# A fused attention and feed-forward kernel: the first two units' scores by head, on 64 rows each, into two PSUM banks, from one smaller load each

## The chip, the core and the metric

The kernel runs on one core of a Trainium2 chip. The core has five engines that run side by side: TensorE for matrix products (PE in the profile, PEld for its loading of the stationary operand), VectorE (DVE), ScalarE (ACT), GpSimd (POOL), and SyncE (SP), whose queue issues nearly all transfers here. Sixteen DMA engines move data between the device memory and SBUF, the on-chip memory. TensorE writes its results into PSUM, eight banks of 512 fp32 numbers on each of 128 partitions; VectorE and ScalarE read them from there.

The metric is the device time of one execution in microseconds (us).

## The reference

Two parts, one after the other. Local attention with memory keys: 4 x 8 heads of 768 tokens and 64 features; each chunk of 32 queries sees 16 tokens to the left of the chunk, the chunk, 8 to the right, and 8 memory keys, so 64 keys.

```python
for c in range(nc):
    ...
    k_full = np.concatenate([mem_k, k_ctx], axis=2)
    v_full = np.concatenate([mem_v, v_ctx], axis=2)
    scores = scale * np.matmul(q_c, k_full.transpose(0, 1, 3, 2))
    scores = scores - np.max(scores, axis=-1, keepdims=True)
    a = np.exp(scores)
    a = a / (np.sum(a, axis=-1, keepdims=True) + 1e-09)
    out[:, :, c_start:c_end] = np.matmul(a, v_full)
```

Then a feed-forward layer over the 3072 tokens of 512 features, with a hidden width of 2048:

```python
h = x @ w_in
g = np.maximum(h, 0.0) + alpha * np.minimum(h, 0.0)
return (g @ w_out).astype(np.float32)
```

All in fp32. At the two ends of a sequence the missing neighbours are left out of the context.

## The kernel before

**Units.** The attention is cut into 32 units: a unit is 384 tokens (half of a sequence, twelve chunks of 32 queries) of one pair of heads. Units 0 to 3 are the four pairs of the first 384 tokens, units 4 to 7 those of the next 384; a unit of the first kind has 16 keys to the left of its first chunk that do not exist, one of the second kind 8 to the right of its last.

**The feed-forward part** works on seven blocks of 384 or 512 tokens. For each block and each of 16 slices of the hidden width (`f`) it multiplies up into `h_ps` (`up`, L741), bends (`below`, `bend`, `high`, `low`) and multiplies down into `o_ps` (`down`, L771). Weights come as 512 KB loads per slice and side and are decoded on ACT, DVE and POOL into a high and a low part (`decode_part`, L638 to L667), since every product is made of three fp32r products. Blocks 0 and 1 are taken in turns while the weights arrive.

**The front.** The first eight units have a path of their own, `windows(u)`: products of queries and keys into PSUM (`score_products`, L317), then on DVE the mask of the missing keys (a memset to -3e38, L520 or L522), the maximum (L524), the subtraction into `e` (L528); the exponential on ACT (L532); the sum and its inverse on DVE (L536, L539); the weights on POOL into `ew` (L549, L553); the turn by TensorE transposes (L561), two copies on ACT (L566), the products with the values (`values`, L574), and the split into a high and a low part (L479 on ACT, L482 on DVE), which are the `up` products' operands. Later units go through `head_products` (L342), which takes the two heads apart: 48 matmuls of 64 rows, two heads in two banks.

In `score_products` one matmul serves both heads: 32 query columns on 128 rows against 2 x 64 keys, where each head's keys are zero on the other head's rows. So a unit's tile `early` is laid out with the keys of one head, the queries, the keys of the other, and it must hold zeros beside the keys. For unit 0 the zeros come with the load, `whole`, 736 KB. For units 1 to 7 they are written by memsets at the start (L211 on POOL, L212 on DVE), and each head comes as a load of 232 KB, `heads`. The values follow as a load of 256 KB each.

**Fillers.** `stir` (L304) issues bf16 products on a constant tile into the unit's score bank ahead of the scores: 8 for unit 0, 2 each for units 1 and 2.

**PSUM.** The eight banks are tiles of pools, allocated anew for each use under a tag: `h0`, `h1`, `o0`, `o1`, `o2`, `s0`, `s1`, `a`. Unit u of the front has its scores in bank `s0` or `s1`, its values' products in `a` or `o2`.

**The order** on each engine is worked out when the program is built, by a list scheduler (`Plan`). Each step has an engine, an estimated cost, what it reads and writes, and a latest-start measure (`rest`); among the steps that could start next on an engine, the one with the longest work behind it goes first. `SHIFT` adds a number of microseconds to that measure for single steps, by their number: a positive one makes the step more urgent. The numbers count the steps in the order in which they are added: the loads of the eight units first (with `al` and `rise`, the slopes' small load and the tile 1 - alpha), then the weights of slices 0 to 7, then the windows of the eight units with 14 steps each, then the rest. On SP a step is a load, so the order among loads comes from there as well.

Of the kernel before, what the change touches and what calls it, by code (L numbers as in the profile page):

```python
# [18 lines left out]
P = 128  # L19
# [82 lines left out]
FIRST_FRONT = 12  # L102


STIR = (8, 2, 0, 0)

DUE_WEIGHTS, LAST_OUT = 4, 8

# [7 lines left out]

NAPART = 2


GATHER_ACT, HIGH_ACT = range(2, 14), 24  # L120


SHIFT = {9: -2.0, 11: 0.6, 18: -3.9, 21: -5.1, 24: 1.4, 25: 3.7, 54: -1.6, 82: 5.1, 87: 1.5, 94: -7.3, 108: 9.2, 136: -11.9, 183: -7.7, 189: -8.2, 192: -9.9, 210: 5.4, 227: 0.7, 228: 3.4}


class Plan:
# [55 lines left out]


@with_exitstack
def body(ctx: ExitStack, tc: tile.TileContext, qvw, kw, whole, heads, w_in, w_out, alpha, out):
    nc = tc.nc
    ctx.enter_context(tc.manual_schedule())
    NKB, NPT, NA = 2, 2, 2
# [11 lines left out]
    ps_h = ctx.enter_context(tc.tile_pool(name="ps_h", bufs=1, space=bass.MemoryType.PSUM))  # L200
    ps_o = ctx.enter_context(tc.tile_pool(name="ps_o", bufs=1, space=bass.MemoryType.PSUM))
    ps_s = ctx.enter_context(tc.tile_pool(name="ps_s", bufs=1, space=bass.MemoryType.PSUM))
    ps_a = ctx.enter_context(tc.tile_pool(name="ps_a", bufs=1, space=bass.MemoryType.PSUM))

    al = const.tile([P, NF], F32, name="al")
    rise = const.tile([P, NF], F32, name="rise")
    busy = const.tile([P, DM], BF16, name="busy")
    nc.vector.memset(busy, 1.0)
    early = [wps[NF - NSET + i, 0].tile([P, NHEAD + NKEYS + NV], F32, name="early", tag="w") for i in range(NSET)]
    for t in early[1:]:  # L210
        nc.gpsimd.memset(t[:, :NKEYS], 0.0)  # L211
        nc.vector.memset(t[:, NHEAD:NHEAD + NKEYS], 0.0)  # L212
    qk = [const.tile([P, BT + NT * NKT], F32, name=f"qk{i}") for i in range(NKB)]
# [92 lines left out]
    def score_products(u):  # L306
        blk, pr = divmod(u, NPAIR)
        st = state[u]
        s_ps = ps_s.tile([P, 512], F32, name="s_ps", tag=f"s{u % 2}")
        stir(s_ps, STIR[0] if u == 0 else STIR[1] if u < 3 else STIR[2])  # L310
        st["s"] = s_ps[:, :2 * NJ * KW].rearrange("p (n k) -> p n k", k=KW)
        t = early[u % NSET]
        q = t[:, NKEYS:NHEAD].rearrange("p (c q) -> p c q", q=CH)
        for j in range(NJ):
            for t4 in range(NT):
                keys = t[:, t4 * NKT + STARTS_WIN[j]:]
                nc.tensor.matmul(  # L317
                    out=st["s"][t4 * CH:(t4 + 1) * CH, 2 * j:2 * j + 2],
                    lhsT=q[:, t4 * NJ + j],
                    rhs=bass.AP(keys.tensor, keys.offset, [keys.ap[0], (NHEAD, 2), (1, KW)]),  # L320
                    start=True, stop=True,
                )

    def banks(us):

        n = len(us)
        ss = [ps_s.tile([P, 512], F32, name="s_ps", tag=f"s{h2}")[:, :n * NJ * KW].rearrange("p (u n k) -> p u n k", u=n, n=NJ)
              for h2 in range(2)]
# [98 lines left out]
    def bank(u):  # L427


        h2 = u % 2  # L430
        if u >= NU - 2:
            return ps_s, f"s{h2}", ("s", h2)
        if h2 or u >= 6 * NPAIR:
            return ps_h, f"h{h2}", f"h{h2}"
        return ps_a, "a", "a"

    def value_products(u):
        st = state[u]
        pool, tag, _ = bank(u)
        st["a"] = pool.tile([P, 512], F32, name="a_ps", tag=tag)  # L440
        for t in range(NT):
            for h2 in range(2):
                nc.tensor.matmul(  # L443
                    out=st["a"][h2 * D:(h2 + 1) * D, t * TQ:(t + 1) * TQ],
                    lhsT=st["v"][:, t, h2, :],
                    rhs=pts[u % NPT][:, :, t, h2, :],
                    start=True, stop=True,
                )
# [41 lines left out]
    def load_first(u):  # L490
        blk, pr = divmod(u, NPAIR)
        t = early[u % NSET]

        def load_whole():
            nc.sync.dma_start(out=t[:, :NHEAD + NKEYS], in_=whole)

        def load_head(h2):
            nc.sync.dma_start(out=t[h2:P:2, h2 * NKEYS:h2 * NKEYS + NHEAD], in_=heads[u, h2])

        def load_values():  # L500
            nc.sync.dma_start(out=t[:, NHEAD + NKEYS:], in_=qvw[blk, pr, :, BT:])

        state[u] = {}
        if u == 0:
            step(SP, 1.88, load_whole, writes=[("fk", u % NSET, 0), ("fk", u % NSET, 1)], rest=due(u))
        else:
            for h2 in range(2):
                step(SP, 0.62, partial(load_head, h2), writes=[("fk", u % NSET, h2)], rest=due(u))
        step(SP, 0.78, load_values, writes=[("fv", u % NSET)], rest=due(u))

    def windows(u):
# [4 lines left out]

        def top():
            s = st["s"]
            if u // NPAIR % 2 == 0:
                nc.vector.memset(s[0:CH, 0:2, 0:LEFT], NEG)  # L520
            else:
                nc.vector.memset(s[3 * CH:4 * CH, 2 * NJ - 2:2 * NJ, KW - NM - RIGHT:KW - NM], NEG)  # L522
            st["mx"] = sm.tile([P, NJ * 2, 1], F32, name="mx", tag=f"mx{u % 3}")
            nc.vector.tensor_reduce(out=st["mx"], in_=s, axis=AX.X, op=ALU.max)  # L524

        def less():
            st["e"] = es[u % 2][:, :, :KW]
            nc.vector.tensor_tensor(out=st["e"], in0=st["s"], in1=st["mx"].broadcast_to([P, NJ * 2, KW]),  # L528
                                    op=ALU.subtract)

        def exps():
            nc.scalar.activation(out=st["e"], in_=st["e"], func=AF.Exp, scale=SCALE)  # L532
# [7 lines left out]

        def scale(part):

            e = st["e"].rearrange("p (j h) k -> p h j k", h=2)
            den = st["den"].rearrange("p (j h) x -> p h j x", h=2)
            ew = ews[u % NPT]
            if part == 0:
                out = ew.rearrange("p h j k -> p h (j k)")[:, :, :2 * (P + CH)]
                out = out.rearrange("p h (j k) -> p h j k", j=2)[:, :, :, :KW]
                nc.gpsimd.tensor_tensor(out=out, in0=e[:, :, :2], in1=den[:, :, :2].broadcast_to([P, 2, 2, KW]),  # L549
                                        op=ALU.mult)  # L550
                return
            for lo, hi, at_ in ((0, KW - NM, P - KW + NM), (KW - NM, KW, CH)):
                nc.gpsimd.tensor_tensor(out=ew[:, :, 2, at_:at_ + hi - lo], in0=e[:, :, 2, lo:hi],  # L553
                                        in1=den[:, :, 2].broadcast_to([P, 2, hi - lo]), op=ALU.mult)
# [11 lines left out]
            nc.scalar.copy(out=et[:, h2], in_=st["t"][h2][:, :NJ * P])  # L566

        def values():
            pool, tag = (ps_o, "o2") if u % 2 else (ps_a, "a")
            st["a"] = pool.tile([P, 512], F32, name="a_ps", tag=tag)  # L570
            v = early[u % NSET][:, NHEAD + NKEYS:].rearrange("p (t h d) -> p t h d", t=NT, h=2)
            for t in range(NT):
                for h2 in range(2):
                    nc.tensor.matmul(  # L574
                        out=st["a"][h2 * D:(h2 + 1) * D, t * TQ:(t + 1) * TQ],
                        lhsT=v[:, t, h2, :],
                        rhs=st["et"][:, h2, :, t, :],
                        start=True, stop=True,
                    )
# [3 lines left out]
        step(DVE, 0.66, top, writes=[sk, ("mx", u % 3)])  # L583
        step(DVE, 0.55, less, reads=[sk, ("mx", u % 3)], writes=e_keys(u))
# [119 lines left out]
    def hidden(blk, f, first_f, last_f):  # L704
# [219 lines left out]
    plan.send()  # L924


_ORDER = ["qvw", "kw", "whole", "heads", "w_in", "w_out", "alpha"]


def _layout(q, k, v, mem_k, mem_v, moe_w_in, moe_w_out, moe_alpha):  # L930
# [7 lines left out]
    def keys(x, mem, s, *spans):  # L938
# [42 lines left out]
```

## Time and profile before

| | |
|---|---|
| device time, median of 3 runs | 597.28 us (596.87 to 597.48) |
| the profiled execution's own time | 596.39 us |
| its span, first to last instruction | 594.5 us |
| granted TensorE clock, mean | 0.999 |
| busy, share of the span | PE 99%, PEld 85%, DVE 66%, ACT 35%, POOL 8% |
| chain that ended last, by engine | PE 96%, DVE 2%, issue 1%, POOL 1% |
| moved by DMA | 47.65 MB, mean 80 GB/s |
| DMA's share by fortieths of the span, the first five | 0.8, 0.9 or more, 0.9 or more, 0.9 or more, 0.3 |

How to read it. A row of a group or of the timeline names a line of the kernel, an engine, an operation, and output and input by the program's names; a row of the chain of work gives start, length, and what ran. Busy time is engine time; what stands in brackets behind a timeline row is how long the engine was idle before it and what ended that. Waits are inferred from semaphores, POOL's spans are rough, and a few records of matmuls can be missing.

### The profile page before, as it was taken

The numbers are of one execution on the slowest core, as the hardware profiler recorded it, in microseconds if no ns is written. First come the engines' busy times: TensorE is split into PE (matmuls) and PEld (weight loads), VectorE is DVE, ScalarE is ACT, GpSimd is POOL, SyncE is SP. The second block draws the span as 40 slices with busy tenths as digits, with TensorE's granted clock in tenths as the row PEclk, the third lists the DMA queues.
The fourth block names the chain that finished last, engine by engine and source line by source line (L and its number), as shares of the span: only waits on it lengthen the run. The fifth ranks groups of instructions, "written<-read, shape, count | busy, mean of one in ns | idle before, by whom it ended". The sixth has DMA issues, their size and how long they took to land.

```text
span 594.5 us, 10993 instructions
## 1 busy us (share of the span) xinstructions
PE 587.2 (99%) x4411; PEld 503.1 (85%) x4412; DVE 391.3 (66%) x907; ACT 208.1 (35%) x578; POOL 48.4 (8%) x74
## 2 busy tenths in 40 slices
PE   7999999999999999999999999999999999999997
PEld 4789998888998989989898888888888888888886
DVE  7989899787869768686895842851961771530530
ACT  3778788625131504424224202302400401210201
POOL 5740000011000101010010100100100100000000
PEclk9999999999999999999999999999999999999999
DMA  8999300222040211403304003003101000000001
GB/s 319 388 408 407 130 0 2 66 65 89 2 153 18 85 59 43 153 1 101 101 0 154 1 1 100 2 0 120 53 1 36 0 1 36 36 1 0 2 0 71
DMA packets 21187, 47.65 MB, mean 80 GB/s; under 512 B 2576, under 2 KB 5904, under 8 KB 21136
## 3 DMA queue, kind: packets, MB, share of 16 engines
q1 hardware_dynamic: 20992, 46.83, 22.1%
q8 instruction: 34, 0.56, 0.4%
q14 instruction: 17, 0.14, 0.1%
q10 hardware_dynamic: 144, 0.13, 0.1%
HBM read 40.66 MB, written 6.29 MB: 79 GB/s over the span
## 4 chain that ended last, share of the span: by engine, by line
PE 96%; DVE 2%; issue 1%; POOL 1%; ACT 0%; POOLq 0%; ACTq 0%
PE h_ps L741 45%; PE o_ps L771 44%; PE a_ps L443 3%; PE s_ps L342 2%; PE s_ps L304 1%; PE a_ps L574 1%; DVE den L536 0%; DVE mx L524 0%; POOL ew L553 0%; PE s_ps L317 0%; DVE e L528 0%; PE o_ps L561 0%; POOL ew L549 0%; DVE w_t L646 0%; DVE a L654 0%
## 5 line engine op out<-in xcount | busy, mean ns | idle before, releaser
L741 PE MATMUL h_ps<-xh,w 128*128 128x384 f32 (+1 forms) x896 | 248.9, 359 | 0.0
L741 PEld LDWEIGHTS h_ps<-xh,w 128*128 128x128 f32 x896 | 164.9, 188 | 16.0
L771 PE MATMUL o_ps<-w,gh 128*128 128x512 f32 x528 | 162.8, 390 | 0.0
L741 PE MATMUL h_ps<-xl,w 128*128 128x384 f32 (+1 forms) x448 | 162.6, 363 | 0.0
L750 ACT ACTIVATE g<-h_ps 128x384 f32<-128x384 f32 (+1 forms) x112 | 60.5, 540 | 195.1 <-PE h_ps L741 128.3
L753 DVE SCALAR_TENSOR_TENSOR g<-g,rise,h_ps 128x384 f32<-128x384 f32 (+1 forms) x112 | 74.7, 668 | 73.1 <-ACT g L750 72.2
L771 PEld LDWEIGHTS o_ps<-w,gh 128*128 128x128 f32 x528 | 99.1, 188 | 20.4
L418 DVE STREAM_TRANSPOSE pt<-e 32x192 f32<-32x192 f32 (+1 forms) x336 | 99.4, 301 | 7.5 <-POOL e L397 2.0
L771 PE MATMUL o_ps<-w,gl 128*128 128x512 f32 x264 | 102.9, 390 | 0.0
L741 PEld LDWEIGHTS h_ps<-xl,w 128*128 128x128 f32 x448 | 84.1, 188 | 10.0 <-DVE xl L482 0.2
L771 PE MATMUL o_ps<-w,xh 128*128 128x512 f32 x240 | 74.9, 393 | 0.0
L771 PEld LDWEIGHTS o_ps<-w,gl 128*128 128x128 f32 x264 | 49.6, 188 | 10.2
L482 DVE TENSOR_TENSOR xl<-a_ps,xh 128x384 fp32r<-128x384 f32 x32 | 17.6, 555 | 59.9 <-ACT xh L479 59.2
L397 POOL TENSOR_TENSOR e<-e,den 128x384 f32<-128x384 f32 x24 | 22.3, 930 | 406.8 <-DVE den L394 267.9
L771 PEld LDWEIGHTS o_ps<-w,xh 128*128 128x128 f32 x240 | 45.0, 188 | 8.9
L759 DVE CAST gh<-g 128x512 fp32r<-128x512 f32 (+1 forms) x72 | 29.0, 403 | 30.7 <-PE o_ps L771 28.1
L479 ACT CAST xh<-a_ps 128x384 fp32r<-128x384 f32 x32 | 14.9, 481 | 95.9 <-PE a_ps L443 93.5
L763 DVE TENSOR_TENSOR gl<-g,gh 128x512 fp32r<-128x512 f32 (+1 forms) x72 | 46.9, 653 | 1.7
L771 PE MATMUL o_ps<-w,xl 128*128 128x512 f32 x120 | 46.8, 390 | 0.0
L376 ACT ACTIVATE e<-s_ps,mx 128x64 f32<-128x64 f32 x144 | 43.2, 317 | 9.6 <-DVE mx L368 9.6
L376 ACT ACTIVATION_READ_ACCUMULATOR e<-s_ps,mx 128x1 f32 x144 | 30.4, 211 | 0.0
L828 ACT COPY o_t<-o_ps 128x512 f32<-128x512 f32 x21 | 12.2, 588 | 44.6 <-PE o_ps L771 44.2
(61 smaller groups left out, 384.4 us busy)
## 6 DMA issues: line engine op xcount, KB each, us to landing
w_t<-w_in SPq DMA_DIRECT2D x16, 512.0 KB, 10.1
w_t<-w_out SPq DMA_DIRECT2D x16, 512.0 KB, 10.2
qk<-kw SPq DMA_DIRECT2D x24, 272.0 KB, 4.3
v_t<-qvw SPq DMA_DIRECT2D x24, 256.0 KB, 2.8
out<-o_t SPq DMA_DIRECT2D x23, 256.0 KB, 2.0
qk<-qvw SPq DMA_DIRECT2D x24, 192.0 KB, 4.6
early<-heads SPq DMA_DIRECT2D x14, 232.0 KB, 4.8
early<-qvw SPq DMA_DIRECT2D x8, 256.0 KB, 5.7
```

Source lines behind the costliest of these rows:

```text
L376: nc.scalar.activation(out=st["e"][:, i], in_=st["s"][h2][:, n], func=AF.Exp, scale=SCALE, bias=d["mx"][:, u - us[0], n, h2:h2 + 1], accum ...
L397: nc.gpsimd.tensor_tensor(out=st["e"], in0=st["e"], in1=st["den"].broadcast_to([P, NJ * 2, KW]), op=ALU.mult)
L418: nc.vector.transpose(out=pts[u % NPT][quad * CH:(quad + 1) * CH, j, t0:t0 + n1 - n0].rearrange("p t h q -> p (t h) q"), in_=(st["e"], zer ...
L443: nc.tensor.matmul(out=st["a"][h2 * D:(h2 + 1) * D, t * TQ:(t + 1) * TQ], lhsT=st["v"][:, t, h2, :], rhs=pts[u % NPT][:, :, t, h2, :], sta ...
L479: nc.scalar.copy(out=ring[k][0][:, cols], in_=st["a"][:, :BT])
L482: nc.vector.tensor_tensor(out=ring[k][1][:, cols], in0=st["a"][:, :BT], in1=ring[k][0][:, cols].bitcast(F32), op=ALU.subtract)
L741: nc.tensor.matmul(out=h["ps"][:, :n_cols], lhsT=ws[f, 0][:, wk, k * P:(k + 1) * P], rhs=parts(blk, k)[1](xk), start=(k == 0 and n == 0), ...
L750: nc.scalar.activation(out=h["g"], in_=h["ps"][:, :n_cols], func=AF.Relu, scale=-1.0)
L753: nc.vector.scalar_tensor_tensor(out=h["g"], in0=h["g"], scalar=rise[:, f:f + 1], in1=h["ps"][:, :n_cols], op0=ALU.mult, op1=ALU.add)
L759: copy(out=h["gh"], in_=h["g"])
L763: nc.vector.tensor_tensor(out=h["gl"], in0=h["g"], in1=h["gh"].bitcast(F32), op=ALU.subtract)
L771: nc.tensor.matmul(out=o_ps[tt], lhsT=h[gk][:, tt * P:(tt + 1) * P], rhs=ws[f, 1][:, wk], start=(f == first_f and i == 0), stop=(f == last ...
```

## The change

Units 0 and 1 get scores by head. Their tile holds queries (384 columns) and keys (544 columns) of head 0 on rows 0 to 63 and of head 1 on rows 64 to 127, in one load of 464 KB each (`firsts`); no zeros are needed, so the two memsets for unit 1's tile go. `pair_products` runs 48 matmuls on 64 rows, head h of unit u into bank u + 2h of one tile.

That tile, `sums`, keeps four banks for the whole program in place of the tags `s0`, `s1`, `a` and `o2`; the pool `ps_a` is gone. So the scores of unit 0 lie in the banks 0 and 2 (formerly `s0` and `a`), those of unit 1 in 1 and 3 (`s1` and `o2`). The mask of the missing left keys is written into all four banks once, before anything else, and the matmuls of a unit's first chunk leave these 16 columns alone; so units 0 and 1 have no memset ahead of their maximum. In `e`, heads now come outermost, for all eight units of the front.

The fillers go to bank `h0`, and unit 0 has five in place of eight. `rise` is computed on POOL in place of DVE. The list of shifts is a new one; as steps are counted, unit 1 has one step fewer, so the same step's number is lower by one. Counted in the new numbers: the weights of slice 0 (24, 25) and the first of slice 1 (26) get +4.3, +3.2, +2.1, where before only the first had one, of +3.7; the values of units 3, 4 and 5 (11, 14, 17) get -4.2, -3.1, -2.5, where before those of units 2, 5 and 6 had -2.0, -3.9, -5.1. The others are for single steps of the windows, of the decode and of the first slices.

```diff
-STIR = (8, 2, 0, 0)
+STIR = (5, 2, 0, 0)
...
+NAPAIR = 2
...
-SHIFT = {9: -2.0, 11: 0.6, 18: -3.9, 21: -5.1, 24: 1.4, 25: 3.7, 54: -1.6, 82: 5.1, 87: 1.5, 94: -7.3, 108: 9.2, 136: -11.9, 183: -7.7, 189: -8.2, 192: -9.9, 210: 5.4, 227: 0.7, 228: 3.4}
+SHIFT = {11: -4.2, 14: -3.1, 17: -2.5, 24: 4.3, 25: 3.2, 26: 2.1, 86: -13.2, 112: 3.2, 187: 3.3, 191: -8.6, 205: 8.0, 218: 1.7, 219: -1.3, 235: -2.0, 241: 8.2}
...
-    ps_a = ctx.enter_context(tc.tile_pool(name="ps_a", bufs=1, space=bass.MemoryType.PSUM))
...
-    for t in early[1:]:
+    sums = ps_s.tile([P, 4, DM], F32, name="sums")
+    S0, S1, A, O2 = range(4)
+    nc.vector.memset(sums[0:CH, :, :LEFT], NEG)
+    for t in early[NAPAIR:]:
         nc.gpsimd.memset(t[:, :NKEYS], 0.0)
         nc.vector.memset(t[:, NHEAD:NHEAD + NKEYS], 0.0)
...
     def score_products(u):
         blk, pr = divmod(u, NPAIR)
         st = state[u]
-        s_ps = ps_s.tile([P, 512], F32, name="s_ps", tag=f"s{u % 2}")
-        stir(s_ps, STIR[0] if u == 0 else STIR[1] if u < 3 else STIR[2])
-        st["s"] = s_ps[:, :2 * NJ * KW].rearrange("p (n k) -> p n k", k=KW)
+        num = STIR[0] if u == 0 else STIR[1] if u < 3 else STIR[2]
+        if num:
+            stir(ps_h.tile([P, 512], F32, name="h_ps", tag="h0"), num)
+        if u < NAPAIR:
+            return pair_products(u)
+        s = sums[:, u % 2, :2 * NJ * KW].rearrange("p (n k) -> p n k", k=KW)
+        st["s"] = s.rearrange("p (j h) k -> p h j k", h=2)
...
+    def pair_products(u):
+
+        st = state[u]
+        t = early[u]
+        st["s"] = sums[:, u % 2::2, :NJ * KW].rearrange("p h (j k) -> p h j k", k=KW)
+        for j in range(NJ):
+            for t4 in range(NT):
+                c, k = t4 * NJ + j, BT + t4 * NKT + STARTS_WIN[j]
+                lo = LEFT if c == 0 else 0
+                for h2 in range(2):
+                    rows = slice(h2 * D, (h2 + 1) * D)
+                    nc.tensor.matmul(
+                        out=st["s"][t4 * CH:(t4 + 1) * CH, h2, j, lo:],
+                        lhsT=t[rows, c * CH:(c + 1) * CH],
+                        rhs=t[rows, k + lo:k + KW],
+                        start=True, stop=True,
+                    )
...
-        def load_whole():
-            nc.sync.dma_start(out=t[:, :NHEAD + NKEYS], in_=whole)
+        def load_both():
+            nc.sync.dma_start(out=t[:, :NHEAD], in_=firsts[u])
...
-        if u == 0:
-            step(SP, 1.88, load_whole, writes=[("fk", u % NSET, 0), ("fk", u % NSET, 1)], rest=due(u))
+        if u < NAPAIR:
+            step(SP, 1.2, load_both, writes=[("fk", u % NSET, 0), ("fk", u % NSET, 1)], rest=due(u))
...
-            if u // NPAIR % 2 == 0:
-                nc.vector.memset(s[0:CH, 0:2, 0:LEFT], NEG)
-            else:
-                nc.vector.memset(s[3 * CH:4 * CH, 2 * NJ - 2:2 * NJ, KW - NM - RIGHT:KW - NM], NEG)
+            if u // NPAIR % 2:
+                nc.vector.memset(s[3 * CH:4 * CH, :, NJ - 1, KW - NM - RIGHT:KW - NM], NEG)
+            elif u >= NAPAIR:
+                nc.vector.memset(s[0:CH, :, 0, 0:LEFT], NEG)
...
-            nc.vector.tensor_tensor(out=st["e"], in0=st["s"], in1=st["mx"].broadcast_to([P, NJ * 2, KW]),
-                                    op=ALU.subtract)
+            nc.vector.tensor_tensor(out=st["e"].rearrange("p (h j) k -> p h j k", h=2), in0=st["s"],
+                                    in1=st["mx"].broadcast_to([P, 2, NJ, KW]), op=ALU.subtract)
...
-            pool, tag = (ps_o, "o2") if u % 2 else (ps_a, "a")
-            st["a"] = pool.tile([P, 512], F32, name="a_ps", tag=tag)
+            st["a"] = sums[:, O2 if u % 2 else A]
...
-        step(PE, 1.33 if u < 3 else 0.8, partial(score_products, u), reads=[("fk", u % NSET, h2) for h2 in range(2)], writes=[sk],
+        step(PE, 1.33 if u < 3 else 0.8, partial(score_products, u), reads=[("fk", u % NSET, h2) for h2 in range(2)],
+             writes=[sk] + ([("a", ("o", 2))[u % 2]] if u < NAPAIR else []),
              rest=due(u))
...
-            step(DVE, 0.1, partial(nc.vector.tensor_scalar, out=rise, in0=al, scalar1=-1.0, scalar2=1.0, op0=ALU.mult,
+            step(POOL, 0.2, partial(nc.gpsimd.tensor_scalar, out=rise, in0=al, scalar1=-1.0, scalar2=1.0, op0=ALU.mult,
```

More of the change, by code (lines that the diff above doesn't have):

```diff
@@ L184, in body @@
 @with_exitstack
-def body(ctx: ExitStack, tc: tile.TileContext, qvw, kw, whole, heads, w_in, w_out, alpha, out):
+def body(ctx: ExitStack, tc: tile.TileContext, qvw, kw, firsts, heads, w_in, w_out, alpha, out):
     nc = tc.nc
@@ L317, in score_products @@
                 nc.tensor.matmul(
-                    out=st["s"][t4 * CH:(t4 + 1) * CH, 2 * j:2 * j + 2],
+                    out=s[t4 * CH:(t4 + 1) * CH, 2 * j:2 * j + 2],
                     lhsT=q[:, t4 * NJ + j],
@@ L322, in score_products @@
                 )
+    def pair_products(u):
[14 more added lines that the diff above has]
+                    )
     def banks(us):
         n = len(us)
-        ss = [ps_s.tile([P, 512], F32, name="s_ps", tag=f"s{h2}")[:, :n * NJ * KW].rearrange("p (u n k) -> p u n k", u=n, n=NJ)
+        ss = [sums[:, h2, :n * NJ * KW].rearrange("p (u n k) -> p u n k", u=n, n=NJ)
               for h2 in range(2)]
@@ L431, in bank @@
         if u >= NU - 2:
-            return ps_s, f"s{h2}", ("s", h2)
+            return None, h2, ("s", h2)
         if h2 or u >= 6 * NPAIR:
             return ps_h, f"h{h2}", f"h{h2}"
-        return ps_a, "a", "a"
+        return None, A, "a"
     def value_products(u):
@@ L439, in value_products @@
         pool, tag, _ = bank(u)
-        st["a"] = pool.tile([P, 512], F32, name="a_ps", tag=tag)
+        st["a"] = pool.tile([P, 512], F32, name="a_ps", tag=tag) if pool else sums[:, tag]
         for t in range(NT):
@@ L518, in top @@
             s = st["s"]
-            if u // NPAIR % 2 == 0:
-                nc.vector.memset(s[0:CH, 0:2, 0:LEFT], NEG)
-            else:
-                nc.vector.memset(s[3 * CH:4 * CH, 2 * NJ - 2:2 * NJ, KW - NM - RIGHT:KW - NM], NEG)
-            st["mx"] = sm.tile([P, NJ * 2, 1], F32, name="mx", tag=f"mx{u % 3}")
+            if u // NPAIR % 2:
+                nc.vector.memset(s[3 * CH:4 * CH, :, NJ - 1, KW - NM - RIGHT:KW - NM], NEG)
+            elif u >= NAPAIR:
+                nc.vector.memset(s[0:CH, :, 0, 0:LEFT], NEG)
+            st["mx"] = sm.tile([P, 2, NJ, 1], F32, name="mx", tag=f"mx{u % 3}")
             nc.vector.tensor_reduce(out=st["mx"], in_=s, axis=AX.X, op=ALU.max)
@@ L541, in scale @@
         def scale(part):
-            e = st["e"].rearrange("p (j h) k -> p h j k", h=2)
-            den = st["den"].rearrange("p (j h) x -> p h j x", h=2)
+            e = st["e"].rearrange("p (h j) k -> p h j k", h=2)
+            den = st["den"].rearrange("p (h j) x -> p h j x", h=2)
             ew = ews[u % NPT]
@@ L568, in values @@
         def values():
-            pool, tag = (ps_o, "o2") if u % 2 else (ps_a, "a")
-            st["a"] = pool.tile([P, 512], F32, name="a_ps", tag=tag)
+            st["a"] = sums[:, O2 if u % 2 else A]
             v = early[u % NSET][:, NHEAD + NKEYS:].rearrange("p (t h d) -> p t h d", t=NT, h=2)
@@ L579, in values @@
                     )
-        step(PE, 1.33 if u < 3 else 0.8, partial(score_products, u), reads=[("fk", u % NSET, h2) for h2 in range(2)], writes=[sk],
+        step(PE, 1.33 if u < 3 else 0.8, partial(score_products, u), reads=[("fk", u % NSET, h2) for h2 in range(2)],
+             writes=[sk] + ([("a", ("o", 2))[u % 2]] if u < NAPAIR else []),
              rest=due(u))
-        step(DVE, 0.66, top, writes=[sk, ("mx", u % 3)])
-        step(DVE, 0.55, less, reads=[sk, ("mx", u % 3)], writes=e_keys(u))
+        also = [("a", ("o", 2))[u % 2]] if u < NAPAIR else []
+        step(DVE, 0.56 if u < NAPAIR else 0.66, top, writes=[sk, ("mx", u % 3)] + also)
+        step(DVE, 0.55, less, reads=[sk, ("mx", u % 3)] + also, writes=e_keys(u))
         step(ACT, 0.52, exps, writes=e_keys(u))
@@ L766, in down @@
             if f == first_f:
-                banks = ([(ps_o, f"o{i}") for i in range(NTT)] + [(ps_a, "a")])[:n_tiles] if not joint else [(ps_s, "s0"), (ps_s, "s1"), (ps_a, "a")]
-                o_ps.extend(pool.tile([P, DM], F32, name="o_ps", tag=tag) for pool, tag in banks)
+                banks = [(ps_o, "o0"), (ps_o, "o1"), (None, O2), (None, A)][:n_tiles] if not joint else [(None, S0), (None, S1), (None, A)]
+                o_ps.extend(pool.tile([P, DM], F32, name="o_ps", tag=tag) if pool else sums[:, tag] for pool, tag in banks)
             for tt in tts:
@@ L924, in body @@
     plan.send()
-_ORDER = ["qvw", "kw", "whole", "heads", "w_in", "w_out", "alpha"]
+_ORDER = ["qvw", "kw", "firsts", "heads", "w_in", "w_out", "alpha"]
 def _layout(q, k, v, mem_k, mem_v, moe_w_in, moe_w_out, moe_alpha):
@@ L951, in _layout @@
                       np.concatenate([qfirst[:, 1], kfirst[:, 1]], axis=2)], axis=1)
-    whole = np.zeros((D, 2, NHEAD + NKEYS), q.dtype)
-    for h in range(2):
-        whole[:, h, h * NKEYS:h * NKEYS + NHEAD] = heads[0, h]
+    firsts = np.concatenate([qfirst.reshape(NWIN, P, BT), kfirst.reshape(NWIN, P, NKEYS)], axis=2)[:NAPAIR]
     vparts = vwin.reshape(NHALF, NPAIR, P, NV)
@@ L958, in _layout @@
         kw=np.ascontiguousarray(kwin).reshape(NHALF, NPAIR, P, NT, NKT),
-        whole=whole.reshape(P, NHEAD + NKEYS),
+        firsts=firsts,
         heads=heads,
```

## The prediction, as it was made before the change had run

> **What bounds the kernel now.** I read the page first, then busy times by stage, then the chain of work that ended last over its first 30 us, then the order of time there, and last the loads.
>
> ```profile
> span 594.5 us, 10993 instructions
> ...
> PE 587.2 (99%) x4411; PEld 503.1 (85%) x4412; DVE 391.3 (66%) x907; ACT 208.1 (35%) x578; POOL 48.4 (8%) x74
> ```
>
> ```profile
> 0.00:5.05 5.05, 3.60 (x8) 1.04 (x8) 3.71 (x8) 1.28 (x1) 4.45 (x16) 1.00 0.61 207
> 5.05:10.00 4.95, 4.22 (x91) 2.74 (x96) 3.72 (x12) 1.25 (x3) 1.42 (x3) 1.00 0.98 345
> 10.00:15.00 5.00, 4.03 (x75) 2.91 (x68) 4.46 (x12) 3.10 (x8) 2.32 (x6) 1.00 1.04 408
> 15.00:20.00 5.00, 4.79 (x100) 3.60 (x96) 4.57 (x14) 3.40 (x8) 3.51 (x7) 1.00 1.00 361
> 20.00:25.00 5.00, 4.78 (x74) 4.07 (x65) 4.52 (x12) 3.70 (x9) 4.18 (x9) 1.00 1.02 391
> 25.00:30.00 5.00, 4.86 (x45) 4.17 (x42) 4.90 (x12) 4.72 (x13) 3.74 (x8) 1.00 1.02 412
> 30.00:35.00 5.00, 5.00 (x51) 4.26 (x50) 3.65 (x6) 3.97 (x8) 2.61 (x3) 1.00 1.03 406
> ```
>
> A stage row gives, after the stage and its length, busy time of PE, PEld, DVE, ACT and POOL, then granted clock, DMA share and GB/s. PE idles 594.5 - 587.2 = 7.3 us in all. Of these 1.45 lie in the first stage and 0.73 + 0.97 + 0.21 + 0.22 + 0.14 = 2.27 in the next five; from 30 us on it has no gap, and the other 3.6 us are the last store. What follows the front is a fixed stream of products, so a change to the first units is worth what it lets that stream start sooner, and no more. In the front three things run close together: DMA is full from 5 us on, DVE nine tenths busy from 10 us on, and PE. The chain there:
>
> ```profile
> 1.45 3.60 PE s_ps L304 x8
> 5.06 1.18 PE s_ps L317 x24
> ...
> 7.91 0.34 DVE mx L524
> ...
> 10.74 0.47 DVE mx L524
> ```
>
> PE carries it through the scores of units 0 and 1, then DVE from maximum to maximum.
>
> **The change, part by part.** In order of time, in brackets what the engine waited for; the last row is the load's size and its time from issue to landing.
>
> ```profile
> 0.73 0.38 SPq L495 DMA_DIRECT2D early<-whole  x1
> ...
> 5.06 0.92 PEld L317 LDWEIGHTS s_ps<-early 128*32 128x32 f32 x24 [0.92 <-DMA early<-whole]
> ...
> 6.18 0.61 PE L304 MATMUL s_ps<-busy 128*128 128x512 bf16 x2
> 6.36 0.09 DVE L520 MEMSET s_ps<- 32x32 f32 x1 [0.94 <-PE s_ps L317]
> 6.48 0.56 DVE L524 TENSOR_REDUCE mx<-s_ps 128x6 f32<-128x384 f32 x1
> ...
> 9.61 0.86 PE L317 MATMUL s_ps<-early 128*32 128x128 f32 x24 [0.52 <-DMA early<-heads]
> ...
> 12.46 0.86 PE L317 MATMUL s_ps<-early 128*32 128x128 f32 x24 [0.96 <-DMA early<-heads]
> early<-whole SPq DMA_DIRECT2D x1, 736.0 KB, 4.3
> ```
>
> *The first load* shrinks from 736 to 464 KB, 278.5 thousand bytes less. At the 345 to 412 GB/s of the stages above that is 0.81 to 0.68 us; I take 0.73. It landed at 0.73 + 4.3 = 5.03, and PE's first scores started on it at 5.06; after, they start at 4.33. Bounds: nothing, if start-up and not bytes sets the landing, and 4.3 x 272/736 = 1.59 us, if all of it scales; I keep near the rate, as DMA runs full soon after. The Trainium skill's page "DMA: Bandwidth & Descriptors", section "Anatomy of one DMA — SWDGE (gpsimd) path", has a fit of 2.0 us plus bytes over 436 GB/s. The 4.3 us here is above its 3.7 for 736 KB; by its slope the gain would be an estimated 0.64 in place of 0.73.
>
> *Unit 1's load* has the bytes of its two old ones and goes right behind the first. So all loads behind them, in a full queue, land about 0.73 sooner too, among them those of units 3 and 4, for which PE waited at 9.61 and 12.46.
>
> *The products.* For units 0 and 1, 24 matmuls on 128 rows become 48 on 64 rows. The later units run that form already:
>
> ```profile
> 108.35 1.24 PE L342 MATMUL s_ps<-qk 64*32 64x64 f32 x96
> 109.52 0.45 PE L741 MATMUL h_ps<-xl,w 128*128 128x384 f32 x1
> ...
> L317 PE MATMUL s_ps<-early x192: 271/273/421, 5.1 to 20.0; 128*32 128x128 f32 x192
> L304 PE MATMUL s_ps<-busy x11: 380/634/635, 1.5 to 7.7; 128*128 128x512 bf16 x11
> ```
>
> Two units take 109.52 - 108.35 = 1.17 us, 0.585 each. Unit 0 of the old form took 1.18 where unit 3's took 0.86: its matmuls reach 421 ns against a median of 273, and the fillers 634 against 380, while the granted clock reads 1.00 in these stages. So PE runs slow for its first four us, whatever that column says, and unit 0's 48 matmuls, all of them now in that time, take twice 0.585 = 1.17. Unit 1 takes 0.585 where the old form took about 0.86.
>
> *The mask.* One memset of four banks at the start, ahead of everything and under the wait for the load, replaces the one ahead of unit 0's and of unit 1's maximum (6.36 to 6.48, so 0.12 each). Unit 0's products end at 4.33 + 1.17 = 5.50; with the 0.18 that stands between 6.18 and 6.36 its maximum starts at 5.68 against 6.48: **0.80 us**. For unit 1, DVE does unit 0's maximum and subtraction first (some 0.59 each) until 6.86, while PE does two fillers (0.61) and the products (0.585) by 6.7; so 6.87 against 7.91: **1.04 us**.
>
> *Fillers.* Eight become five, at 0.45 each (3.60 for eight): they end at 3.7, and PE idles 0.6 until the load, which comes last anyway: nothing. Were the load to land before 3.7, they would be what is late next. In bank h0 they wait for no subtraction any more; that gain lies beside DVE's work.
>
> *From unit 2 on* DVE goes on by its own work, 1.04 sooner. Unit 3's scores waited for their load until 9.61 and ended at 10.47, 0.27 ahead of the maximum at 10.74; a load 0.73 sooner so allows 1.0 at most. Unit 4's load allows PE 0.73 at 12.46, and what PE lacks there it makes up from its waits behind, 0.21 us in the next stage. I take **0.95** carried to 20 us; bounds 0.73 and 1.04 by the same rows.
>
> ```profile
> 25.03 0.45 DVE L173 TENSOR_SCALAR rise<-al 128x16 f32<-128x16 f32 x1
> L553 POOL TENSOR_TENSOR ew<-e,den 128x16 f32<-128x16 f32 x8 | 1.9, 232 | 0.0
> ```
>
> *`rise`* leaves DVE (0.45) for POOL, where the row of that size says 0.23. DVE is 98% busy in that stage, but PE lacks only 0.14 us: I take **0.1**, bounds 0.45 and -0.23 (POOL late with the weights for a turn, on which PE waits).
>
> *Memsets of `early`:* one on DVE and one on POOL go, in the time in which DVE came to wait 0.94 for the scores: nothing on the path; they clear the way for unit 2's loads.
>
> *The kept tile, heads outermost in `e`, new operand patterns:* as many elements and instructions as before; zero. A view over banks 0 and 2 could tie unit 0 to bank 1: a rival.
>
> *The shifts* move weights 0 and 1 ahead on SP's queue and the values of units 3, 4 and 5 back; later ones reorder steps of the decode. No row prices an order. I take zero, with up to 1.1 us either way, half of the 2.27 that PE idles.
>
> Sum: 0.95 + 0.1 = 1.05 us. The profiled execution took 596.39 (its span of 594.5 and 1.9 around it), 0.9 under the median of 597.28; I carry the difference over: 597.28 - 1.05 = **596.2**.
>
> **The rivals.**
>
> *More than that (17%).* With loads and DVE ahead, the new order fills half of PE's 2.27 us: 1.05 + 1.1, so 595.1. For it: the waits at 9.61 and 12.46 are for loads, which come sooner. Against: from 15 us on PE lacks only 0.57 us.
>
> *The kept tile ties units together (11%).* If unit 0's reads of banks 0 and 2 are taken to touch bank 1, unit 1's products wait for its subtraction (6.86) and end at 7.45, and the maximum starts at 7.6 against 7.91. Gain 0.3: 597.0. No row bears on how such views are tracked.
>
> *PE stays slow longer (8%).* PE speeds up some 4.2 us after its first filler, all without a pause. Now a pause of 0.6 falls into that time. If full speed then comes 3.4 us later, at about 9.1, unit 1 ends at 5.50 + 0.9 + 1.17 = 7.6 and unit 2, half of it slow, at about 9.6, when its maximum stood before: the gain is gone, 597.3. The Trainium skill's page "TensorE: Matmul & The Clock Gate", section "What's actually happening", says this: half clock until some 3.4 us of sustained work have been seen, in windows that run freely. The slow first matmuls agree; no run here shows how long a pause is forgiven.
>
> *Values late: slower (16%).* Here the queue decides:
>
> ```profile
> 13.02 1.52 SPq L501 DMA_DIRECT2D early<-qvw  x3
> ...
> 23.11 1.35 PEld L574 LDWEIGHTS a_ps<-qk,early 128*64 128x64 f32 x32 [0.25 <-DMA early<-qvw]
> early<-qvw SPq DMA_DIRECT2D x8, 256.0 KB, 5.7
> ```
>
> The three value loads issued from 13.02 land by 14.5 + 5.7 = 20.2, after the change by 19.5, and the products at 23.11 that need them move to 22.1. Each 512 KB of weights put before them costs 1.3 us at 412 GB/s. Two are free; four land them at 24.7, PE stands 2.6 us, and the end is 598.8. It decides from the third weight on. For it: the wait of 0.25 in that row. Against: the values have 2.6 us in hand.
>
> **How the numbers follow.** The forecast has 48%, with a range of its own from 595.5 to 596.9 by the bounds above. A measurement of this kernel tells about 0.2%, 1.2 us, from no change; the forecast lies near that edge, so its chance splits into 24 faster and 24 within. Faster 24 + 17 = 41%; within 0.2% 24 + 11 + 6 = 41%; slower 16 + 2 = 18%. The range of 594.6 to 597.9 reaches past the first rival for the unpriced order and leaves out most of the late values and the far end on both sides, about 2 in 10.
>
> **What would show it.** First scores at about 4.3 (5.06); the first maximum at about 5.7 (6.48), unit 1's at 6.9 (7.91); unit 3's scores at 8.9 (9.61); PE without gaps about 1 us sooner and a span near 593.5. It is wrong if the first load lands near 5 us with fewer bytes, if slow matmuls go on past 6 us, if unit 1's products wait for a subtraction, or if value products wait for their load.

## The result, and the profile after

The changed kernel takes 615.02 us (median of 6 executions, 612.16 to 617.74), the kernel before beside it 596.98 us (596.6 to 597.48): ratio 1.030, 95% interval 1.0266 to 1.0334, so 18.0 us slower. The forecast was 596.2 us. The profiled execution took 612.16. Comparisons here and below leave out executions in which the clock was disturbed for long.

First the head of the page after, and the chain by engine:

```profile
span 610.4 us, 11071 instructions
...
PE 590.4 (97%) x4457; PEld 503.4 (82%) x4457; DVE 388.6 (64%) x904; ACT 209.3 (34%) x578; POOL 48.1 (8%) x74
...
PE 92%; DVE 4%; DMA 2%; ACT 1%; issue 1%; POOL 0%; SPq 0%; DVEq 0%; POOLq 0%; ACTq 0%
```

PE idles 610.4 - 590.4 = 20.0 us where it idled 7.3, and is busy 3.2 us longer; 12.7 + 3.2 make up the 15.9 by which the spans differ. The stages, columns as before:

```profile
0.00:5.05 5.05, 3.40 (x54) 1.44 (x55) 3.65 (x9) 1.28 (x1) 4.45 (x16) 1.00 0.64 212
5.05:10.00 4.95, 3.17 (x76) 1.47 (x74) 2.17 (x7) 0.74 (x2) 0.61 (x1) 1.00 0.99 350
10.00:15.00 5.00, 3.42 (x46) 2.67 (x50) 3.33 (x10) 2.46 (x5) 1.89 (x5) 0.66 1.05 395
15.00:20.00 5.00, 3.54 (x72) 2.47 (x66) 2.99 (x8) 1.89 (x5) 1.92 (x5) 1.00 0.96 347
20.00:25.00 5.00, 3.19 (x56) 2.50 (x54) 3.31 (x8) 2.65 (x6) 1.77 (x4) 1.00 1.04 406
25.00:30.00 5.00, 3.71 (x54) 2.80 (x52) 2.98 (x10) 3.52 (x9) 3.27 (x9) 1.00 1.04 416
30.00:40.00 10.00, 7.96 (x94) 6.59 (x92) 6.85 (x15) 6.31 (x16) 5.39 (x8) 1.00 1.03 406
...
100.00:200.00 100.00, 97.44 (x805) 87.23 (x804) 75.66 (x176) 42.21 (x128) 5.98 (x6) 1.00 0.17 56
...
300.00:400.00 100.00, 98.80 (x798) 83.25 (x797) 66.50 (x177) 28.17 (x107) 5.35 (x6) 1.00 0.18 53
```

In the first 40 us PE idles 11.6 us (before 3.7), and it has gaps of 2.56 and 1.20 where it had none; the last stage adds 1.0. DVE, before nine tenths busy from 10 us on, is down to about 3 us in 5: no compute engine is full, they wait for each other. The stage from 10 to 15 us also shows a granted clock of 0.66; a part of the longer busy time lies there (24 matmuls of 0.86 us take 1.51). The order of time after shows what the engines wait for:

```profile
3.96 0.95 PE L343 MATMUL sums<-early 64*32 64x48 f32 x48 [0.20 <-DVE early L216]
...
5.81 0.95 PE L343 MATMUL sums<-early 64*32 64x48 f32 x48
...
6.80 0.56 DVE L550 TENSOR_REDUCE mx<-sums 128x6 f32<-128x384 f32 x1 [1.72 <-PE sums L343]
...
8.05 0.86 PE L325 MATMUL sums<-early 128*32 128x128 f32 x24 [0.69 <-issue]
8.97 0.56 DVE L550 TENSOR_REDUCE mx<-sums 128x6 f32<-128x384 f32 x1 [1.02 <-PE sums L325]
...
18.13 0.86 PE L325 MATMUL sums<-early 128*32 128x128 f32 x24 [0.81 <-DVE mx L550]
...
19.06 0.48 ACT L505 CAST xh<-sums 128x384 fp32r<-128x384 f32 x1 [1.31 <-PE sums L325]
...
306.05 0.88 PE L469 MATMUL sums<-pt,v_t 128*64 128x96 f32 x16 [1.20 <-DVE mx L391]
```

Unit 0's scores end at 4.91 in banks 0 and 2. Its maximum starts at 6.80, right after *unit 1's* scores end (6.76), in banks 1 and 3. Unit 1's maximum (8.97) waits for unit 2's scores in bank 0 (end 8.91). At 18.13 PE waits for a maximum, at 19.06 ScalarE's cast of a unit's values waits for scores in another bank, and at 306.05, far behind the front, value products wait for a maximum of scores where there was no gap before. All these instructions have one thing in common: the tile `sums`.

### The profile page after: what moved, and what is told of

Read it like the earlier page. It is cut to its first block, busy times and chain, and to the rows that moved or that the text cites. A ratio compares the mean times of both kernels' runs of the same rounds, so it can differ in the third digit from the quotient of the medians.

```text
span 610.4 us, 11071 instructions
## 1 busy us (share of the span) xinstructions
PE 590.4 (97%) x4457; PEld 503.4 (82%) x4457; DVE 388.6 (64%) x904; ACT 209.3 (34%) x578; POOL 48.1 (8%) x74
## 3 DMA queue, kind: packets, MB, share of 16 engines
HBM read 40.38 MB, written 6.29 MB: 76 GB/s over the span
## 4 chain that ended last, share of the span: by engine, by line
PE 92%; DVE 4%; DMA 2%; ACT 1%; issue 1%; POOL 0%; SPq 0%; DVEq 0%; POOLq 0%; ACTq 0%
PE h_ps L768 43%; PE o_ps L798 22%; PE sums L798 20%; PE sums L368 2%; PE a_ps L469 2%; DVE pt L444 1%; PE sums L469 1%; PE sums L599 1%; DMA w_t<-w_in 1%; PE o_ps L587 1%; DVE xl L508 1%; DMA early<-heads 0%; ACT xh L505 0%; PE sums L325 0%; DVE early L216 0%
## 5 line engine op out<-in xcount | busy, mean ns | idle before, releaser
L798 PE MATMUL o_ps<-w,gh 128*128 128x512 f32 x288 | 88.8, 390 | 0.0
L798 PE MATMUL sums<-w,gh 128*128 128x512 f32 x240 | 73.9, 389 | 0.0
L798 PEld LDWEIGHTS o_ps<-w,gh 128*128 128x128 f32 x288 | 54.1, 188 | 11.1
L798 PE MATMUL o_ps<-w,gl 128*128 128x512 f32 x144 | 56.1, 390 | 0.0
L798 PEld LDWEIGHTS sums<-w,gh 128*128 128x128 f32 x240 | 45.0, 188 | 9.4
L402 ACT ACTIVATE e<-sums,mx 128x64 f32<-128x64 f32 x144 | 43.6, 319 | 22.2 <-DVE mx L394 12.3
L798 PE MATMUL sums<-w,gl 128*128 128x512 f32 x120 | 46.8, 390 | 0.7 <-ACT o_t L855 0.7
L798 PE MATMUL o_ps<-w,xh 128*128 128x512 f32 x124 | 38.6, 393 | 0.0
L798 PE MATMUL sums<-w,xh 128*128 128x512 f32 x116 | 36.2, 393 | 0.0
L798 PEld LDWEIGHTS o_ps<-w,gl 128*128 128x128 f32 x144 | 27.0, 188 | 5.6
```

The source lines that it names most:

```text
L402: nc.scalar.activation(out=st["e"][:, i], in_=st["s"][h2][:, n], func=AF.Exp, scale=SCALE, bias=d["mx"][:, u - us[0], n, h2:h2 + 1], accum ...
L798: nc.tensor.matmul(out=o_ps[tt], lhsT=h[gk][:, tt * P:(tt + 1) * P], rhs=ws[f, 1][:, wk], start=(f == first_f and i == 0), stop=(f == last ...
```

## The experiments

Theory: every access to one bank of the kept tile waits for the other engines' earlier accesses to any bank of that tile, all through the program. Rivals: keeping the banks (not allocating them anew) costs; the new shifts bring loads late; fewer fillers leave PE slow.

**1 and 2. The kept banks alone.** In the kernel before, the tags `s0`, `s1`, `a`, `o2` become kept banks, as one tile or as four, and nothing else changes.

```diff
+    kept_sums = ps_s.tile([P, 4, DM], F32, name="sums")        # one tile
+    sums = [kept_sums[:, i] for i in range(4)]
...
+    sums = [ps_s.tile([P, DM], F32, name=f"sums{i}", tag=f"sums{i}") for i in range(4)]   # four tiles
...
-        s_ps = ps_s.tile([P, 512], F32, name="s_ps", tag=f"s{u % 2}")
+        s_ps = sums[u % 2]
```

> The kernel before with one part of the change alone: its banks s0, s1, a and o2 become the four banks of one kept tile. Order, loads, fillers, shifts and products stay. Theory A, one tile: an access to one bank of the tile waits for the accesses of other engines to its other banks. Then 610 to 620 us, PE's idle time in the first 40 us goes from 3.7 to over 8 us, and maxima on DVE wait for scores of the next unit. Rival B, the order: the new shifts cost the time; then 597 within 0.6, as the shifts are the old ones. Rival C, slow PE: five fillers are too few and PE falls back to the slow clock; then 597 within 0.6 as well, as eight fillers stay.

> The same as the run before it, with four kept tiles of one bank each in place of one of four. All three theories expect 597 within 1 us: it tells whether the cost is that tiles are kept for the whole program, or that four banks are one tile. If keeping alone costs, this one is slow too (over 605).

One tile: 614.95 us (three executions, 613.99 to 616.13), ratio 1.0304 (1.0284 to 1.0324). Four tiles: 596.92, ratio 1.0001 (0.9991 to 1.001). As many banks, the same views of single banks, the same order on each engine: 18.0 us lie between one tile and four. Keeping costs nothing, and the change's loss, 18.0 us as well, is there without its products, loads, fillers or shifts. A part of it may come with the clock: the three executions have a mean granted clock of 0.992 to 0.997, and the one of experiment 3, at 0.999, is 16.4 us above the kernel before.

**3. One tile in the kernel before, its profile.**

> The kernel before with its four banks as one kept tile and nothing else changed, once more for a profile of it at full clock. It took 613.99 to 616.13 us. If accesses to one bank wait for other engines' accesses to another bank of the same tile, PE waits in the front ahead of scores for DVE's maxima and subtractions of the unit before and ahead of value products for ScalarE's copies of another unit, PE idles 10 to 20 us more than the 7.3 of the kernel before, and each such wait names an operation on another bank. If the tile instead makes single instructions longer, PE is busy some 15 us more and the waits are those of the kernel before.

613.32 us. The page's head and the order of time in the front of this kernel:

```profile
span 611.5 us, 10985 instructions
...
PE 590.9 (97%) x4412; PEld 502.4 (82%) x4412; DVE 390.7 (64%) x907; ACT 208.9 (34%) x578; POOL 47.8 (8%) x74
```

```profile
5.12 1.17 PE L320 MATMUL sums<-early 128*32 128x128 f32 x24
...
7.07 0.86 PE L320 MATMUL sums<-early 128*32 128x128 f32 x24 [0.25 <-DMA early<-heads]
8.03 0.09 DVE L523 MEMSET sums<- 32x32 f32 x1 [2.60 <-PE sums L320]
...
9.49 0.56 DVE L527 TENSOR_REDUCE mx<-sums 128x6 f32<-128x384 f32 x1
...
10.10 0.59 PE L307 MATMUL sums<-busy 128*128 128x512 bf16 x2 [2.16 <-DVE mx L527]
10.62 0.87 PE L320 MATMUL sums<-early 128*32 128x128 f32 x24
11.55 0.56 DVE L531 TENSOR_TENSOR e<-sums,mx 128x384 f32<-128x384 f32 x1 [1.03 <-PE sums L320]
```

```profile
PE sums L320 <- DVE e L531: 2.7, 2, 1.4
PE h_ps L743 <- DVE xl L485: 2.2, 5, 0.6
PE sums L307 <- DVE mx L527: 2.2, 1, 2.2
...
PE sums L320 <- DVE mx L527: 1.3, 2, 0.8
PE sums L446 <- DVE mx L368: 1.2, 1, 1.2
```

The last fence is the list of PE's waits: for what, us in total, times, the longest. Its second row is a wait for an operand made from the values' products, which come later themselves. Unit 0's mask (8.03) waits until unit 1's scores end (7.93), though its own ended at 6.29. Unit 2's fillers in bank `s0` (10.10) wait until unit 1's maximum in `s1` ends (10.05); unit 1's subtraction (11.55) then waits until unit 2's scores in `s0` end (11.49). Each is a pair of different banks, accessed one bank at a time. PE idles 611.5 - 590.9 = 20.6 us, 13.3 more than in the kernel before. Its busy time is 3.7 us up as well, at full clock. Single matmuls are hardly longer: in the two largest groups the mean is 335 and 389 ns, with four tiles 336 and 390; what makes up the 3.7 us stays open. So the theory holds on waits, and instructions longer by 15 us are ruled out. The profile infers these waits from semaphores, and the two programs of experiments 1 and 2 differ in how banks are grouped into tiles: the order was put into the program when it was built. By which rule stays open.

**4. The whole change with four tiles.** A view now covers one bank only, so units 0 and 1 get a maximum and a subtraction for each bank.

```diff
-    sums = ps_s.tile([P, 4, DM], F32, name="sums")
+    sums = [ps_s.tile([P, DM], F32, name=f"sums{i}", tag=f"sums{i}") for i in range(4)]
...
+            if u < NAPAIR:
+                for h2 in range(2):
+                    nc.vector.tensor_reduce(out=st["mx"][:, h2], in_=s[h2], axis=AX.X, op=ALU.max)
+                return
```

> The changed kernel with four kept tiles of one bank each in place of one of four; order, shifts, loads, fillers stay. Units 0 and 1 have one maximum and one subtraction for each of their two banks, so four short DVE instructions more, some 0.1 us each over the joint ones, and four short memsets in place of one. Theory A: 594.5 to 597, what was forecast for the change within its range. Rival B (shifts): 612 to 618, as after. Rival C (slow PE): over 603, with slow matmuls beyond 8 us.

> The changed kernel with four kept one-bank tiles, once more. It took 595.93 us; eight of its ten executions had a mean granted clock of 0.999 or 1.000 and took 595.59 to 596.33, two had 0.997 and took 597.84 and 598.12. If the rest of the change is worth what the prediction's sum said (1.05 us), the median lies 0.7 to 1.2 us under the kernel before and the executions with the full clock within 595.5 to 596.4; if the first result was chance, at the kernel before or above it. An execution with the lower clock again takes some 2 us more.

595.93 us, ratio 0.999 (0.9979 to 1.0001), and again 596.16, ratio 0.999 (0.9981 to 1.0). The 19 us are gone, and the rest of the change is worth 0.7 to 0.9 us, at the edge of what can be told from nothing.

**5. Which banks share a tile.** Two tiles of one score and one value bank each, as the pairs of the new products need; then only the score banks in one tile; then only the other two.

```diff
+    both = [ps_s.tile([P, 2, DM], F32, name=f"sums{i}", tag=f"sums{i}") for i in range(2)]   # two tiles
+    sums = [both[i % 2][:, i // 2] for i in range(4)]
...
+    pair = ps_s.tile([P, 2, DM], F32, name="sums", tag="sums")      # score banks in one
+    sums = [pair[:, 0], pair[:, 1]]
+    sums += [ps_s.tile([P, DM], F32, name=f"sums{i}", tag=f"sums{i}") for i in (2, 3)]
...
+    sums += [pair[:, 0], pair[:, 1]]                                # value banks in one
```

> The changed kernel with two kept tiles of two banks each: banks 0 and 2 (units 0, 2, 4, 6: scores and values' products of even units) and banks 1 and 3 (odd units). Instructions are those of the changed kernel, but for two mask memsets in place of one. Theory A: a part of the cost stays, as scores of an even unit are still tied to values' products of an even unit, but units 0 and 1 are no longer tied: 600 to 608. Rivals B and C: 612 to 618.

> Four kept banks as in the experiment with four tiles, but the two banks of the scores are one tile; the two others stay tiles of their own. If an access to one bank of a tile waits for accesses of other engines to its other bank, a unit's scores wait until DVE has subtracted the unit before, and in the decode one half's scores wait for the other half's reads: between 598 and 610. The experiment with two tiles, each of one bank of scores and one of values, gave 600.63. If it is not which banks share a tile but that a tile spans four banks, 595.6 to 596.5.

> The mirror of the one with the score banks: the two banks of the scores are tiles of their own, the two others (values of even and of odd units, and down products of the windowed stage) are one tile. If accesses to the two banks of a tile wait for each other, the down products of the windowed stage and the value products of neighbouring units wait for ScalarE's reads: between 596.5 and 602, less than the score banks, since fewer steps touch these two banks close together. If only tiles of four banks are slow, 595.6 to 596.5.

Two tiles 600.63, ratio 1.0067 (1.0051 to 1.0082); score banks 598.35, ratio 1.0029 (1.0018 to 1.004); value banks 599.66, ratio 1.0047 (1.0031 to 1.0062). Every tie costs, so it is not four banks in a tile that are slow. My order was wrong: the value banks cost no less than the score banks, and the intervals overlap. From the four tiles at 0.999, two tied banks cost some 2 to 3.5 us, two such ties 4.6, and the tile of all four 19. The four ties tried, of the six between four banks, add up to some 10; the other two (scores of the one kind with values of the other) were not tried by themselves.

**6. The shifts.** Four tiles with the old list of shifts, renumbered; and four tiles with the new list and unit 4's heads issued ahead of the first weights.

```diff
-SHIFT = {11: -4.2, 14: -3.1, 17: -2.5, 24: 4.3, ...
+SHIFT = {8: -2.0, 10: 0.6, 17: -3.9, 20: -5.1, 23: 1.4, 24: 3.7, ...
...
+SHIFT = {11: -4.2, 14: -3.1, 17: -2.5, 24: 4.3, ..., 12: 2.0, 13: 2.0}
```

> The changed kernel with four kept one-bank tiles, and with the shifts of the kernel before, their numbers less one each for the one step fewer ahead of them; the loads of weights and values so stand on the queue as they did before. With the new shifts, four tiles gave 595.93 (595.59 to 598.12). If the new shifts bring the value loads late (the prediction's slower case), the old ones give about 595 or less. If they are worth nothing, 595.6 to 596.3. If they fit the order to the earlier loads, as their being changed along with the loads would have it, the old ones give 596.5 to 597.5, so that the rest of the change by itself is worth nothing.

> Four kept one-bank tiles, and two shifts more (steps 12 and 13, by 2.0 us), which issue unit 4's two head loads ahead of the first input weights instead of behind them; nothing else on that queue moves. If the wait of unit 4's scores for their load (2.89 us in the profile of the four tiles, a slow execution; 0.96 in the kernel before) holds up the stream of products, the time falls by 0.3 to 0.8 us from 595.93, to 595.1 to 595.6. If PE makes that wait up from its later waits, as the prediction's step for units 3 and 4 had it, 595.7 to 596.2. If the input weights then come late, above 596.5.

Old shifts 596.5, ratio 0.9998 (0.9989 to 1.0007), against 0.999 with the new ones: the new list brings nothing late, and is worth some tenths at most, at the edge of the noise. With the old list the rest of the change can't be told from nothing. Heads first 597.49, ratio 1.0012 (1.0003 to 1.002): worse, in the range that I gave for late weights. Its profile shows three things that no run separates: the first decode step starts at 11.14 in place of 10.19 in the repeated four tiles, behind its weights; PE waits 1.65 us at 9.99 for an earlier load of heads, and 0.74 us at 26.68 for DVE.

**7. Fillers.** In four executions of eleven of the repeated four tiles (and two of the first ten) the mean granted clock was 0.997 and the time 597.05 to 598.12; the others had 0.999 or 1.000 and took 595.59 to 596.35. The profile of the repeat is one with the lower clock:

```profile
10.00:15.00 5.00, 3.07 (x33) 2.23 (x31) 3.64 (x10) 2.84 (x6) 1.96 (x4) 0.70 1.03 395
```

```profile
9.08 1.07 PE L597 MATMUL o_ps<-eye,ew 128*128 128x128 f32 x6
12.09 1.51 PE L326 MATMUL sums<-early 128*32 128x128 f32 x24 [1.93 <-DMA early<-heads]
13.53 1.54 PE L597 MATMUL o_ps<-eye,ew 128*128 128x128 f32 x6
```

PE runs through the front sooner, then waits 1.93 us for unit 4's heads, and the 24 matmuls behind that wait take 1.51 us in place of 0.86. Two edits fill PE's time, one at the wait, one at the start:

```diff
-        num = STIR[0] if u == 0 else STIR[1] if u < 3 else STIR[2]
+        num = STIR[0] if u == 0 else STIR[1] if u < 3 else 3 if u == 4 else STIR[2]
...
-STIR = (5, 2, 0, 0)
+STIR = (8, 2, 0, 0)
```

> Four kept one-bank tiles, and three fillers (matmuls on a constant, about 0.38 us each) ahead of unit 4's scores, where PE waits for their load (1.83 us in the four tiles with the old shifts, 2.89 in the slow profile of the four tiles). If that wait is what makes the granted clock fall in some executions (0.66 to 0.78 from 10 to 15 us), no execution of this kernel shows a mean clock of 0.997, the slow ones at 597.8 to 598.3 are gone, and the median is 595.6 to 596.0. If the pause has nothing to do with it, about one execution in five is slow as before. If the load lands early more often than not, the fillers are in the way and the median rises by up to 0.5 us.

> Four kept one-bank tiles with the eight fillers of the kernel before ahead of unit 0's scores in place of five. They end some 1.1 us later, at about 4.8 in place of 3.7, while the first load lands at about 3.9. If fillers that outlast the load hold up the first scores, the time is 0.5 to 0.9 us above that of the four tiles, 596.4 to 596.9. If the pause between the fillers and the scores matters (PE slow for longer after it), keeping PE busy gives that back: 595.6 to 596.2. No step of the prediction gave the fillers a price; it named this as what is late next.

Three fillers ahead of unit 4: 595.64 us (595.36 to 596.62), ratio 0.9979 (0.997 to 0.9988). Eight for unit 0: 595.74 (595.4 to 596.61), ratio 0.998 (0.9971 to 0.9989). In none of the 22 executions is the clock below 0.999. Both are faster than the kernel before by 1.1 to 1.2 us, and than the changed one by 19. They are no faster than the four tiles at full clock (595.59 to 596.35): what the fillers take away is the executions at the lower clock. The span, the stage and the order of time of the first:

```profile
span 593.5 us, 11075 instructions
```

```profile
10.00:15.00 5.00, 3.97 (x75) 2.75 (x72) 3.96 (x11) 3.72 (x8) 2.54 (x6) 1.00 1.05 404
```

```profile
4.04 0.94 PE L344 MATMUL sums<-early 64*32 64x48 f32 x48 [0.27 <-DVE early L217]
...
5.03 0.35 DVE L553 TENSOR_REDUCE mx<-sums 128x3 f32<-128x192 f32 x1
...
5.46 0.70 PE L344 MATMUL sums<-early 64*32 64x48 f32 x48
...
6.18 0.62 DVE L553 TENSOR_REDUCE mx<-sums 128x3 f32<-128x192 f32 x2
...
7.35 0.86 PE L326 MATMUL sums<-early 128*32 128x128 f32 x24 [0.65 <-DMA early<-heads]
8.49 0.86 PE L326 MATMUL sums<-early 128*32 128x128 f32 x24 [0.28 <-DVE sums L549]
...
10.00 0.81 PE L309 MATMUL h_ps<-busy 128*128 128x512 bf16 x3
11.84 0.86 PE L326 MATMUL sums<-early 128*32 128x128 f32 x24 [1.03 <-DMA early<-heads]
...
16.66 0.87 PE L326 MATMUL sums<-early 128*32 128x128 f32 x24
```

With eight fillers for unit 0 the first scores start at 4.98, hardly sooner than before (5.06):

```profile
4.98 0.95 PE L344 MATMUL sums<-early 64*32 64x48 f32 x48
...
11.41 0.87 PE L326 MATMUL sums<-early 128*32 128x128 f32 x24 [0.38 <-DVE e L564]
```

The end comes as soon all the same, with unit 4's scores at 11.41 in place of 12.46: the gain does not hang on how soon the first scores start. I expected a loss of 0.5 to 0.9 if these fillers outlast the load; they do, and it costs nothing. Nor is it shown that a pause ahead of the first scores slows PE: unit 0's products take 0.95 us here and 0.94 behind five fillers.

## Why the prediction was wrong

**The step that failed** is "*The kept tile, heads outermost in `e`, new operand patterns:* as many elements and instructions as before; zero". The elements and instructions are the same; what changed is which of them wait for which. That term measured 18.0 us by itself (experiments 1 and 2).

**The rival** named the right object, and was priced from one place. It took a view over banks 0 and 2 to touch bank 1, and let unit 1's products wait for unit 0's subtraction, gain 0.3. Neither held: the tie needs no such view (in experiment 1 each access covers one bank), and it works both ways, in the order of the program: unit 0's maximum waited for unit 1's products. Above all, it shows at waits of PE, DVE and ScalarE through the whole program, and not at one place in the front: at 306.05 us, and at 604.36, where a down product into `sums` waits 0.72 us for ScalarE's copy. Once a tie was thought possible, it should have been followed through every user of the tile. A sign of this kind was listed, "if unit 1's products wait for a subtraction"; what showed was the reverse, unit 0's maximum waiting 1.72 us for unit 1's products.

**The other steps** can be read from the four tiles with three fillers ahead of unit 4, whose profile shows a span of 593.5, against "near 593.5". That the number comes so near is in part luck: steps missed both ways, and with eight fillers the first scores start 0.08 us sooner in place of 0.73 while the time is 1.1 us shorter all the same. Which of the steps brings the gain stays open.

- *The first load* was mis-sized, on the safe side: 

```profile
early<-firsts SPq DMA_DIRECT2D x1, 464.0 KB, 3.1
```

  This row is of the changed kernel. It lands at 0.73 + 3.1 = 3.83, 1.20 sooner than before, where 0.73 was taken and 1.59 was the bound. By the fit that the Trainium skill's page "DMA: Bandwidth & Descriptors" gives in "Anatomy of one DMA — SWDGE (gpsimd) path", 464 KB take an estimated 3.1 us. The fit is for loads issued by GpSimd, this one is SyncE's; the trace agrees with it here, and was above it for 736 KB.
- *The products*: unit 0's 48 matmuls took 0.94 (1.17 forecast), unit 1's 0.70 (0.585).
- *The mask and the maxima*: the first maximum at 5.03 (5.7 forecast, 6.48 before), unit 1's at 6.18 (6.9, 7.91), both by halves; unit 3's scores at 8.49 (8.9, 9.61).
- *Carried on*: unit 1's maximum is 1.73 us sooner. Unit 2's scores, which wait 0.65 for their load, are 0.87 sooner (7.35 against 8.22), unit 3's 1.12, and unit 4's, behind 1.03 of waiting, 0.62 (11.84 against 12.46), less than the 0.73 that their load was to allow. Two units later it is 0.91:

```profile
17.57 0.86 PE L317 MATMUL s_ps<-early 128*32 128x128 f32 x24
```

  This row of the kernel before stands against 16.66. So near 20 us, for which 0.95 was taken with bounds of 0.73 and 1.04, the step's figure comes out, though waits for loads and not the maxima set the pace in between.
- *`rise`* takes 0.20 on POOL in the changed kernel:

```profile
27.69 0.20 POOL L175 TENSOR_SCALAR rise<-al 128x16 f32<-128x16 f32 x1
```

  Its gain was not measured by itself.
- *Shifts*: a few tenths, within the bound of 1.1; *values late* did not occur.
- *Fillers: nothing*: wrong in a way that I had not seen. *PE stays slow longer* looked for a pause at 4 us; the slow matmuls came behind the pause ahead of unit 4's scores that the earlier front opens. 6 of 21 executions of the four tiles show the lower clock (two of them are profiled) and took 1.3 to 2.4 us more than the middle one of the others (595.76).

## What to carry to other kernels

Before banks that were separate allocations become one tile, list who touches each of them on which engine: a whole tile can be the unit by which accesses are ordered. Here waits of up to 2.6 us at many of its users left PE idle for 13 us more and cost 18. Splitting a tile is then the first thing to try, even where it doubles some instructions: two maxima of 0.35 us each in place of one of 0.56 were cheaper by far than the tie. And when a front is made faster, look where its engine now waits: the gain may open a pause in which TensorE's clock is lowered.

## What was not expected of the hardware

After a pause of 1.93 us on PE (experiment 7) the stage from 10 to 15 us shows a granted clock of 0.70, and the 24 matmuls of a unit's scores take 1.51 us in place of 0.86; after 1.03 us, behind three fillers, it stays at 1.00. But the kernel before with one tile paused 2.16 us at 10.10 and its next 24 matmuls took 0.87. And a pause of 1.65 us was followed by 0.87 with unit 4's heads first (at 9.99), and by 1.51 in the changed kernel:

```profile
10.56 1.51 PE L325 MATMUL sums<-early 128*32 128x128 f32 x24 [1.65 <-issue]
```

So the length of the pause alone does not decide. The Trainium skill's page "TensorE: Matmul & The Clock Gate", section "What's actually happening", says that the clock is halved after an idle window of about 3.4 us, and that these windows run freely. All pauses here are shorter than such a window, so the rule as it stands does not give the slow rows. If a window that is idle in part were enough, where the pause falls would decide; no run here moved the pause to test that.
